# Another order for the hand-written list of four engines: the way back and the first two tiles

## The chip, the cores and the metric

One NeuronCore of a Trainium2 chip runs the kernel. The metric is device time in microseconds (us), the median of several runs. TensorE (PE) multiplies, ScalarE (ACT) and VectorE (DVE) read PSUM and do the elementwise work, GpSimd (POOL) works on SBUF alone, and SyncE (SP) issues the DMAs.

## The reference

A block of two layers on `x` of 2048 x 512, float32: a filter in the frequency domain, then a gated MLP, both with a LayerNorm ahead and a residual.

```python
X = rfft2(layernorm(x)) * (w_r + 1j * w_i)
h = x + irfft2(X, (2048, 512))
g, u = layernorm(h) @ w_gate, layernorm(h) @ w_up     # 512 x 1376 each
out = h + (gelu(g) * u) @ w_down                      # 1376 x 512
```

## The kernel before

The two Fourier transforms are matrix products with tables of sines and cosines. A first stage (to about 32 us) takes the LayerNorm and the transform over the sequence, a second (to about 75 us) does the transform over the columns, the filter and half of the way back; it leaves its result in the SBUF tile `gh`, 16 blocks of 128 rows. A third stage, the subject here, takes the blocks through the rest of the way back and begins the MLP. The MLP then runs in 22 tiles (two halves of the rows, 11 slices of 128 of the 1376 hidden columns, the last one padded), and the products with `w_down` are put between them. TensorE is to be fed all the time.

Products of the MLP are made by a scheme with seven products in place of eight (as Strassen's), and each product is three passes in `fp32r` of 2 x 128 rows (lines 100 to 102: high by high, high by low, low by high parts). So activations (`cb`) and weights (`gu`, `wd`) lie in SBUF as a high and a low part.

In the third stage the order of the instructions on PE, ACT, DVE and POOL is written out by hand. `FIRST` is a list of 292 words; each word is one step, and a loop issues them in the order of the list:

```python
with tc.manual_schedule(engines={et.PE, et.Activation, et.DVE, et.Pool}):
    for op in FIRST.split():
        name, *place = op.split(".")
        do[name](*map(int, place))
```

Each engine runs its own steps in the list's order and waits by semaphores for what it needs of the others. SP's DMAs are not in the list. The number behind the dot is a PSUM bank (of eight) or a spare row in SBUF. The names, with a block `b` or a pair `i` of blocks (i and i+4):

| step | engine, line | what it does |
|---|---|---|
| `U b`, `C b`, `V b`, `X b`, `M b` | PE 524, ACT 844 (811 for b over 7), DVE 852, POOL 881, PE 862 (859/860 for b = 3, 7) | a block's way back: product over the columns, copy out, fold by sum and by difference, product over the sequence |
| `O b`, `H b`, `G b`, `I b` | ACT 867, DVE 873, POOL 877 | half of it copied out, residual, the two halves of the block put together |
| `S b`, `A b`, `E i`, `Q i`, `N i`, `R i` | DVE 514, 516, 895, ACT 908, DVE 900 to 902, ACT 906 | second LayerNorm of a pair |
| `T i0`, `T i1`, `a i` to `o i` | PE 557, 563; ACT 568 to 579, DVE 576, 582, POOL 576, 582 | transposes, and the sums, differences, high and low parts in `cb` that the seven products need |
| `K b` | POOL 818 to 821 | a later block unfolded, four instructions |
| `g n h P0` to `P6` | PE 100 to 102 | the seven products of tile n (0, 1), half h (a: pairs 0, 1; b: pairs 2, 3), 256 columns wide |
| `g n h c1, c2, c3` | ACT 660 | copies of the sum so far, between the products that add to it |
| `d1, d2, dy` / `G0, G1` / `m0, m1` / `i0, i1` / `o0, o1` | DVE 663 / ACT 666 / DVE 669 / ACT 675 / DVE 682 | sums, gelu, gate times up, high and low part for the next product |
| `g n awh`, `g n awl` | ACT 503, POOL 505 | high and low part of a slice of `w_down`, behind a DMA into `wdr` |
| `r0` to `r3`, `hc`, `lo1` to `lo3` | POOL 138 to 146, DVE 153, POOL 156 | weights of tile 2: four sums in `raw`, the high part of all of it, the low part in three pieces |
| `g2P0` | PE | the first product of tile 2, 512 columns wide |

A tile holds its three running sums x, y, z in three banks: tile 0 in banks 0 to 2, tile 1 in 3 to 5, tile 2 again in 0 to 2. P0 starts x and `c1` copies it; P2, P4 and P5 add to x, and each waits until the copy before it (`c1`, `c2`, `c3`) has read x. `dy` adds `c3`'s copy and z to y, and P6 adds to z behind it. The pair's transposes T20, T21, T30, T31 go through banks 6, 7, 7 and 5, which other steps use before and after.

Of the kernel before, what the change touches and what calls it, by code (L numbers as in the profile page):

```python
# [31 lines left out]
BY_THEN = (8, 12, 9)  # L32

FIRST = """
u4.0 u0.1 w4 C4.0 w0 C0.1 U1.2 U5.3 V4.2 X4 V0.3 C1.4 V1.0 C5.5 X0 M4.1 V5.1 X1 O4.0 X5 M0.2 H4 U2.3 O0.1 G4 I4
M5.1 C2.5 H0 V2.3 G0 S4 U7.2 M1.3 O5.0 A4 U6.0 I0 U3.4 X2 H5 C7.1 S0 O1.1 A0 H1 M2.1 C6.0 Q0 C3.5 E0.5 N0 G5
U12.3 R01 V7.4 I5 T01.2 G1 I1 V6.3 S5 X7 A5 R00 T00 S1 O2.1 M7.0 X6 s0.0 A1 a0 Q1 l0 V3.1 E1.6 c0 d0 f0 b0 U8.4
U9.7 N1 e0.1 m0 g0 H2 h0 R10 k0 T10 R11 H7 n0 T11.1 X3 a1 s1.2 b1 c1 i0 d1 j0 l1 M3.2 C8 S7 g0aP0 o0 M6.4 e1.0
h1 f1 U14.5 k1 C12 i1 m1 n1 O6.0 g1 g0ac1 U15.3 H3 j1 S3 C15 r0 o1 A3 g0aP1 C9 A7 g0aP2 Q3 C14 G2 H6 g0ac2 E3.7 I2
N3 g0aP3 G6 U10.4 g0aP4 R31 S2 I6 R30 g0ad1 g0ac3 A2 S6 T31.5 A6 T30 s3.6 g0aP5 g1aP0 a3 Q2 E2.6 g0ady c3 C10  # L40
g0aP6 d3 b3 N2 f3 r1 g1ac1 g3 e3.4 K9.5 g1aP1 R20 r2 h3 g1aP2 i3 g1ad1 g1aP3 k3 R21 j3 T20 T21.7 g1ac2 a2 b2
s2.8 c2 g1aP4 g1ac3 l3 g1aP5 g0bP0 K12.4 d2 m3 g0ad2 n3 f2 g1ady g1aP6 e2.7 g2 g0bP1 o3 k2 l2 m2 g0bc1 h2 n2 i2
g0bd1 j2 g0bP2 g0bP3 g0bc2 o2 g1aG0 r3 g0awh K8.4 g0bP4 U11.6 g0bc3 g1am0 g0bG0 g0bdy g0bP5 g0bm0 g0aG0 g1ad2
g0am0 g1bP0 g0aG1 g0bP6 g0am1 g1bP1 g1bc1 g1ai0 g1aG1 g0bd2 g0awl hc g0bi0 g1bP2 g1bc2 g1bd1 g0bo0 g1bP3 g0ai0
g1bP4 g0bG1 g1bc3 g0ai1 g1bP5 g0ao0 g1ao0 lo1 g0bm1 g0ao1 g2P0 g1awh g0bi1 g1bdy g0bo1 g1am1 g1bP6 lo2 g1bG0
g1ai1 g1bm0 g1bd2 g1ao1 g1awl g1bG1 lo3 g1bm1 g1bi0 g1bo0 g1bi1 g1bo1 U13.7 C11 C13
"""

SECOND = """
# [1121 lines left out]
```

## Time and profile before

| | |
|---|---|
| median of 3 runs | 454.15 us (454.14 to 454.22) |
| the profiled execution's own time | 454.05 us |
| its span, first to last instruction | 452.3 us |
| granted TensorE clock, mean | 0.998 |
| PE, PEld, DVE, ACT, POOL busy | 97%, 82%, 61%, 45%, 61% of the span |

The profiled execution is 0.10 us below the median, and 1.75 us of it lie outside the span. The third stage runs from 75.8 us (the first `U`) to 127.9 us (the end of `U13`, the last PE step of the list). A row of the timeline gives the start, the duration, the engine, the line, the operation, and in brackets the idle time ahead of it with what ended it. Matmuls are pipelined, so the distance from one start to the next, not the duration, is what one costs on PE.

### The profile page before, as it was taken

Reading aid. Unit: us, or ns where it says so; the run is one execution under the profiler, and the core shown is the slowest. Engines: PE = TensorE matmul, PEld = TensorE weight load, DVE = VectorE, ACT = ScalarE, POOL = GpSimd, SP = SyncE. Lnnn points to the kernel's source line nnn. Section 1 sums busy time; section 2 is a strip of 40 time slices with the busy share of each in tenths; the row PEclk is TensorE's granted clock in tenths of the full one; section 3 lists DMA queues with packets and bytes.
Section 4 is the critical chain, followed back from the end, with each engine's and each line's share of the span. In section 5 each row is a group of like instructions: output and inputs, shape, how many; then the busy total and the mean of one; then the engine's idle time right before and its main releaser. Section 6 shows DMA issues by size and latency. Waiting matters only on the chain.

```text
span 452.3 us, 6433 instructions
## 1 busy us (share of the span) xinstructions
PE 437.8 (97%) x2289; PEld 371.1 (82%) x2289; DVE 277.1 (61%) x514; ACT 205.6 (45%) x433; POOL 276.5 (61%) x306
## 2 busy tenths in 40 slices
PE   3999999999999999999999999999999999999996
PEld 3999999798878777877888888888888888888875
DVE  5957895797574766358735578266555345635453
ACT  4979785688731242033332765252243034303420
POOL 6986896878859578748662543165566636653210
PEclk9999999999999999999999999999999999999999
DMA  8994805200032022112210213121022102210013
GB/s 288 390 400 147 278 13 179 100 23 1 25 116 93 26 69 93 48 46 71 70 48 23 70 48 116 49 91 46 26 70 71 46 24 71 70 46 25 23 70 118
DMA packets 21168, 41.05 MB, mean 91 GB/s; under 512 B 2064, under 2 KB 7696, under 8 KB 21008
## 3 DMA queue, kind: packets, MB, share of 16 engines
q1 hardware_dynamic: 20992, 40.51, 26.3%
q8 instruction: 18, 0.29, 0.3%
q10 hardware_dynamic: 144, 0.13, 0.1%
q14 instruction: 14, 0.11, 0.1%
HBM read 36.44 MB, written 4.19 MB: 90 GB/s over the span
## 4 chain that ended last, share of the span: by engine, by line
PE 90%; DVE 3%; ACT 2%; DMA 2%; POOL 1%; issue 1%; SPq 0%; POOLq 0%; DVEq 0%
PE ps L756 26%; PE ps L100 15%; PE ps L102 14%; PE ps L101 14%; PE ps L288 4%; PE ps L416 3%; PE ps L427 3%; PE ps L454 3%; PE ps L524 3%; PE ps L862 1%; PE ps L971 1%; DMA gh<-in_x 1%; POOL gu L156 1%; PE ps L563 1%; DMA raw<-in_wgu 1%; PE ps L557 1%
## 5 line engine op out<-in xcount | busy, mean ns | idle before, releaser
L100 PE MATMUL ps<-cb,gu 128*128 128x512 f32 (+1 forms) x336 | 127.9, 381 | 2.0 <-ACT s L660 1.6
L756 PE MATMUL ps<-wd,a 128*128 128x512 f32 (+1 forms) x537 | 125.9, 388 | 0.2 <-DVE gh L759 0.2
L102 PE MATMUL ps<-cb,gu 128*128 128x512 f32 (+1 forms) x336 | 125.0, 372 | 0.0
L101 PE MATMUL ps<-cb,gu 128*128 128x512 f32 (+1 forms) x336 | 124.9, 372 | 0.0
L756 PEld LDWEIGHTS ps<-wd,a 128*128 128x128 f32 x537 | 99.4, 188 | 21.9 <-DVE gh L972 1.0
L156 POOL TENSOR_TENSOR gu<-raw,gu 128x768 fp32r<-128x768 f32 (+1 forms) x54 | 78.3, 1479 | 39.6 <-DVE gu L153 33.4
L660 ACT ACTIVATE s<-ps 128x512 f32<-128x512 f32 (+1 forms) x72 | 40.4, 560 | 133.8 <-PE ps L102 133.5
L100 PEld LDWEIGHTS ps<-cb,gu 128*128 128x128 f32 x336 | 63.3, 188 | 14.9 <-ACT s L660 2.2
L101 PEld LDWEIGHTS ps<-cb,gu 128*128 128x128 f32 x336 | 63.3, 188 | 11.7 <-issue 1.0
L102 PEld LDWEIGHTS ps<-cb,gu 128*128 128x128 f32 x336 | 63.3, 188 | 11.0
L762 DVE TENSOR_TENSOR gh<-ps,gh 128x512 f32<-128x512 f32 x48 | 33.1, 691 | 53.7 <-PE ps L756 53.5
L505 POOL TENSOR_TENSOR wd<-wdr,wd 128x512 fp32r<-128x512 f32 x22 | 28.4, 1291 | 51.3 <-ACT wd L503 51.2
L669 DVE TENSOR_TENSOR ps<-ps,s 128x512 f32<-128x512 f32 (+1 forms) x48 | 31.0, 650 | 24.4 <-PE ps L102 22.2
L675 ACT ACTIVATE a<-ps 128x512 fp32r<-128x512 f32 (+1 forms) x48 | 26.9, 561 | 39.0 <-DVE ps L669 38.6
L682 DVE TENSOR_TENSOR a<-ps,a 128x512 fp32r<-128x512 f32 (+1 forms) x48 | 30.8, 641 | 11.5 <-ACT a L675 9.8
L663 DVE TENSOR_TENSOR s<-ps,s 128x512 f32<-128x512 f32 (+1 forms) x48 | 30.9, 643 | 10.6 <-PE ps L102 9.1
L666 ACT ACTIVATE s<-s 128x512 f32<-128x512 f32 (+1 forms) x48 | 28.2, 592 | 18.4 <-DVE s L663 18.4
L138 POOL TENSOR_TENSOR raw<-raw 128x256 f32<-128x256 f32 x20 | 14.7, 737 | 33.9 <-DMA raw<-in_wgu 32.4
L663 DVE TENSOR_TENSOR ps<-ps,s 128x512 f32<-128x512 f32 (+1 forms) x24 | 15.7, 654 | 27.8 <-ACT s L660 27.8
L288 PE MATMUL ps<-ms,pn 128*128 128x128 f32 x120 | 17.0, 291 | 7.9 <-ACT ms L256 7.8
L288 PEld LDWEIGHTS ps<-ms,pn 128*128 128x128 f32 x120 | 15.6, 205 | 8.3 <-POOL pn L263 7.2
L153 DVE CAST gu<-raw 128x1792 fp32r<-128x1792 f32 x18 | 19.6, 1091 | 3.8 <-PE ps L101 2.9
(126 smaller groups left out, 609.5 us busy)
## 6 DMA issues: line engine op xcount, KB each, us to landing
raw<-in_wgu SPq DMA_DIRECT2D x40, 256.0 KB, 3.1
wt<-in_w SPq DMA_DIRECT2D x16, 520.0 KB, 5.7
wdr<-in_wd SPq DMA_DIRECT2D x22, 256.0 KB, 2.7
out<-gh SPq DMA_DIRECT2D x15, 256.0 KB, 2.0
gh<-in_x SPq DMA_DIRECT2D x7, 512.0 KB, 8.1
row<-in_x SPq DMA_DIRECT2D x12, 256.0 KB, 3.0
mis<-in_mi SPq DMA_DIRECT2D x1, 1024.0 KB, 10.6
a<-in_x SPq DMA_DIRECT2D x4, 256.0 KB, 4.9
```

What stands on the lines that cost most here:

```text
L100: pe.matmul(o, lh, rh, start=(i == 0 and not onto), stop=False, skip_group_check=True)
L101: pe.matmul(o, lh, rl, start=False, stop=False, skip_group_check=True)
L102: last = pe.matmul(o, ll, rh, start=False, stop=(i == n - 1), skip_group_check=True)
L156: pooled["lo"] = pool.tensor_tensor(r[:, 1, m], t[:, m], r[:, 0, m].bitcast(F32), op=ALU.subtract)
L288: pe.matmul(pt[:, c], o, mc, start=(z == 0), stop=(z == len(parts[b][c]) - 1))
L505: pool.tensor_tensor(r[:, 1], t, r[:, 0].bitcast(F32), op=ALU.subtract)
L660: return lambda: act.activation(to, a, AF.Copy)
L663: return lambda: dve.tensor_tensor(to, a, b, op=ALU.add)
L669: return lambda: dve.tensor_tensor(u, u, g, op=ALU.mult)
L682: dve.tensor_tensor(a[:, 1], u, a[:, 0].bitcast(F32), op=ALU.subtract)
L756: pe.matmul(o, parts_of[tiles.index((q, f))][:, ha, i // 4, r], wds[f][:, hw, c], start=start, stop=stop)
L762: dve.tensor_tensor(gh[:, b, c], o, gh[:, b, c], op=ALU.add)
```

## The change

Only the list `FIRST` changes: the same 292 words, with the same banks and rows behind the dots, in another order. Its first and its last rows:

```diff
-u4.0 u0.1 w4 C4.0 w0 C0.1 U1.2 U5.3 V4.2 X4 V0.3 C1.4 V1.0 C5.5 X0 M4.1 V5.1 X1 O4.0 X5 M0.2 H4 U2.3 O0.1 G4 I4
+u4.0 u0.1 w4 C4.0 w0 C0.1 U1.2 C1.4 U5.3 V4.2 X4 V0.3 X0 V1.0 X1 C5.5 V5.1 X5 r0 M4.1 O4.0 M0.2 O0.1 H4 G4 U2.3 C2.5
...
-g1ai1 g1bm0 g1bd2 g1ao1 g1awl g1bG1 lo3 g1bm1 g1bi0 g1bo0 g1bi1 g1bo1 U13.7 C11 C13
+g0bG1 g0bm1 U11.6 C11 g1bP5 g1ao0 g1bP6 g1bd2 g0bi1 g0bo1 g1bG1 U13.7 C13 g2P0 g1bm0 g1bi0 g1bm1 g1bi1 g0ao1 g1bo0
+g1bo1 g1ao1
```

On PE the order of the products from the first of them on was, and is now (the steps with P; with U, T and M between):

```
before: g0aP0 M6 U14 U15 g0aP1 g0aP2 g0aP3 U10 g0aP4 T31 T30 g0aP5 g1aP0 g0aP6 g1aP1 g1aP2 g1aP3 T20 T21 g1aP4 g1aP5
        g0bP0 g1aP6 g0bP1 g0bP2 g0bP3 g0bP4 U11 g0bP5 g1bP0 g0bP6 g1bP1 g1bP2 g1bP3 g1bP4 g1bP5 g2P0 g1bP6 U13
after:  U15 T10 M6 T11 M3 g0aP0 U14 U10 g0aP2 g0aP1 g1aP0 g0aP4 T31 g1aP2 T30 g1aP1 g1aP4 g0aP3 g0aP5 T20 g1aP5 T21 g0aP6
        g0bP0 g1bP1 g1bP0 g1aP3 g0bP1 g0bP2 g1aP6 g0bP3 g0bP4 g1bP2 g0bP5 g0bP6 g1bP3 g1bP4 U11 g1bP5 g1bP6 U13 g2P0
```

ACT, around the loading of the table for gelu (line 666's first row). `s1_907`, `s2_908`, `s3_909` are the copies of tile 0, `s1_910`, `s2_911` those of tile 1; `wd` is the high part of `w_down`; before:

```order
L660 ACTIVATE s1_907<-ps_72 128x256
L579 ACTIVATE cb_885<-row_893 128x2x128
L579 ACTIVATE cb_885<-ps_72 128x2x128
L660 ACTIVATE s2_908<-ps_72 128x256
L666 ACT_TABLE_LOAD
L666 ACTIVATE s1_910<-s1_910 128x256
L503 ACTIVATE wd_1331<-wdr_1329 128x512
L660 ACTIVATE s3_909<-ps_72 128x256
L666 ACTIVATE s1_907<-s1_907 128x256 x2
```

and now:

```order
L660 ACTIVATE s1_907<-ps_72 128x256
L579 ACTIVATE cb_885<-row_892 128x2x128
L666 ACT_TABLE_LOAD
L666 ACTIVATE s1_907<-s1_907 128x256
L660 ACTIVATE s2_908<-ps_72 128x256
L666 ACTIVATE s2_908<-s2_908 128x256
L579 ACTIVATE cb_885<-ps_72 128x2x128
L579 ACTIVATE cb_885<-row_894 128x2x128
L666 ACTIVATE s2_911<-s2_911 128x256
L660 ACTIVATE s3_909<-ps_72 128x256
```

The load now stands ahead of `g0bc2` (`s2_908`) and no longer between it and `g0bc3` (`s3_909`); `g0awh` (`wd`) has left this place for one 59 steps earlier in ACT's order (behind `O1`).

POOL, at the end of the list. `cb` are the steps `m` and `o`, `wd` is `g0awl` or `g1awl`, `gu` are `lo1` to `lo3`, the four rows with `gh` are `K8`; before:

```order
L576 TENSOR_TENSOR row_893<-row_894 128x256
L582 TENSOR_TENSOR cb_885<-row_894,cb_885 128x2x128
L582 TENSOR_TENSOR cb_885<-row_893,cb_885 128x2x128
L146 TENSOR_TENSOR raw_915<-raw_915 128x256
L818 TENSOR_TENSOR row_893<-gh_58 128x2x128
L819 TENSOR_TENSOR row_893<-gh_58 128x2x128
L820 TENSOR_TENSOR gh_58<-row_893 128x256
L821 TENSOR_TENSOR gh_58<-row_893 128x256
L505 TENSOR_TENSOR wd_1331<-wdr_1329,wd_1331 128x512
L156 TENSOR_TENSOR gu_82<-raw_915,gu_82 128x256
L156 TENSOR_TENSOR gu_82<-raw_915,gu_82 128x768
L505 TENSOR_TENSOR wd_1434<-wdr_1432,wd_1434 128x512
```

and now:

```order
L146 TENSOR_TENSOR raw_915<-raw_915 128x256
L582 TENSOR_TENSOR cb_885<-row_893,cb_885 128x2x128
L818 TENSOR_TENSOR row_893<-gh_58 128x2x128
L819 TENSOR_TENSOR row_893<-gh_58 128x2x128
L820 TENSOR_TENSOR gh_58<-row_893 128x256
L821 TENSOR_TENSOR gh_58<-row_893 128x256
L582 TENSOR_TENSOR cb_885<-row_892,cb_885 128x2x128
L582 TENSOR_TENSOR cb_885<-row_894,cb_885 128x2x128
L505 TENSOR_TENSOR wd_1372<-wdr_1370,wd_1372 128x512
L156 TENSOR_TENSOR gu_82<-raw_915,gu_82 128x256
L156 TENSOR_TENSOR gu_82<-raw_915,gu_82 128x768 x2
```

`m3` and `m2`, the low parts that P6 of half b needs, now stand behind `K8`; `g1awl` stands ahead of all three low parts of tile 2's weights.

DVE, around the high part of tile 2's weights (the CAST, `hc`); before:

```order
L669 TENSOR_TENSOR ps_72<-ps_72,s1_907 128x256
L669 TENSOR_TENSOR ps_72<-ps_72,s2_908 128x256
L663 TENSOR_TENSOR s2_908<-ps_72,s2_908 128x256
L153 CAST gu_82<-raw_915 128x1792
L663 TENSOR_TENSOR s1_910<-ps_72,s1_910 128x256
L682 TENSOR_TENSOR a_1388<-ps_72,a_1388 128x256 x2
```

and now:

```order
L669 TENSOR_TENSOR ps_72<-ps_72,s1_910 128x256
L669 TENSOR_TENSOR ps_72<-ps_72,s1_907 128x256
L153 CAST gu_82<-raw_915 128x1792
L669 TENSOR_TENSOR ps_72<-ps_72,s2_911 128x256
L663 TENSOR_TENSOR s2_908<-ps_72,s2_908 128x256
L669 TENSOR_TENSOR ps_72<-ps_72,s1_907 128x256
L663 TENSOR_TENSOR ps_72<-ps_72,s3_912 128x256
```

`hc` now stands ahead of `g0bd2` (`s2_908`), and `g1bdy` (`s3_912`), for which `g1bP6` waits, four steps behind it. `hc` writes over the weights of tile 0, so it can start only behind `g0bP6`, in both orders.

More of the change, by code (lines that the diff above doesn't have):

```diff
@@ L34 @@
 FIRST = """
-u4.0 u0.1 w4 C4.0 w0 C0.1 U1.2 U5.3 V4.2 X4 V0.3 C1.4 V1.0 C5.5 X0 M4.1 V5.1 X1 O4.0 X5 M0.2 H4 U2.3 O0.1 G4 I4
[L36 to L44, printed above, removed]
@@ L45 @@
-g1bP4 g0bG1 g1bc3 g0ai1 g1bP5 g0ao0 g1ao0 lo1 g0bm1 g0ao1 g2P0 g1awh g0bi1 g1bdy g0bo1 g1am1 g1bP6 lo2 g1bG0
-g1ai1 g1bm0 g1bd2 g1ao1 g1awl g1bG1 lo3 g1bm1 g1bi0 g1bo0 g1bi1 g1bo1 U13.7 C11 C13
+u4.0 u0.1 w4 C4.0 w0 C0.1 U1.2 C1.4 U5.3 V4.2 X4 V0.3 X0 V1.0 X1 C5.5 V5.1 X5 r0 M4.1 O4.0 M0.2 O0.1 H4 G4 U2.3 C2.5
+M5.1 I4 O5.0 H0 U7.2 G0 C7.1 V2.3 M1.3 I0 O1.1 S4 g0awh X2 H5 G5 A4 S0 A0 E0.5 Q0 U3.4 C3.5 H1 U6.0 C6.0 M2.1 N0 R00
+R01 U12.3 C12 V7.4 I5 S5 A5 V6.3 U8.4 I1 G1 O2.1 T00 a0 S1 T01.2 A1 Q1 E1.6 X7 M7.0 U9.7 H2 N1 s0.0 c0 d0 C8 R10 g0awl
@@ new lines @@
+H7 e0.1 k0 n0 b0 h0 f0 g0 R11 S7 X6 U15.3 V3.1 X3 l0 i0 j0 T10 a1 b1 I2 G2 m0 M6.4 O6.0 T11.1 s1.2 c1 d1 C15 o0 C9 f1
+e1.0 k1 n1 H6 I6 M3.2 g0aP0 H3 g0ac1 o1 l1 U14.5 C14 m1 U10.4 C10 g1 g0aP2 g0aP1 S3 A3 A7 Q3 g1aP0 h1 i1 g0ac2 g0aP4
+E3.7 N3 R31 T31.5 G6 S6 g1ac1 g1aP2 K12.4 R30 T30 K9.5 S2 A2 g1aP1 A6 E2.6 Q2 s3.6 N2 c3 d3 g1ac2 g1aP4 g0aP3 R21 a3
+e3.4 g0ac3 j1 g0aP5 R20 T20 g1ac3 g1aP5 b3 h3 i3 g0ad1 g1ad1 j3 k3 T21.7 r1 r2 g0ady g0aP6 a2 b2 g0bP0 g1bP1 n3 s2.8
+c2 d2 f3 g3 e2.7 k2 n2 h2 f2 g2 g1bP0 g1bc1 g1aP3 g1ady g0bc1 l3 o3 g0bP1 g0bd1 g0bG0 g0bP2 g0bc2 g0ad2 r3 g1aP6 g1ad2
@@ L47 @@
+g0aG1 g0bP3 i2 j2 g0am1 l2 g1aG1 o2 g0bP4 g0bc3 g0bdy K8.4 g1bd1 g1aG0 g1bP2 g1bc2 g1awh g1am0 g1ai0 g0bP5 g0bm0 g0bi0
+m3 m2 g0bP6 g1bP3 g1bG0 g1awl hc lo1 lo2 lo3 g0aG0 g1am1 g0bd2 g1bP4 g1bc3 g0am0 g0ai0 g0ai1 g1bdy g0ao0 g0bo0 g1ai1
+g0bG1 g0bm1 U11.6 C11 g1bP5 g1ao0 g1bP6 g1bd2 g0bi1 g0bo1 g1bG1 U13.7 C13 g2P0 g1bm0 g1bi0 g1bm1 g1bi1 g0ao1 g1bo0
+g1bo1 g1ao1
 """
```

## The prediction

> **What bounds the kernel now.** I read the page first, then the busy time by stretches, then the timeline of PE in the third stage, and last that of the engines it waits for.
>
> ```profile
> PE 437.8 (97%) x2289; PEld 371.1 (82%) x2289; DVE 277.1 (61%) x514; ACT 205.6 (45%) x433; POOL 276.5 (61%) x306
> 75.70:128.00 52.30, 50.14 (x364) 44.68 (x364) 37.71 (x97) 38.08 (x90) 41.34 (x54) 1.00 0.17 55
> 140.00:450.00 310.00, 308.56 (x1373) 253.57 (x1371) 172.72 (x281) 105.84 (x194) 164.80 (x164) 1.00 0.19 60
> ```
>
> PE is the bound, and behind the changed stretch it is idle for 1.4 us of 310. So what PE gains or loses up to 128 us reaches the end of the span, and a reordering can win only what PE loses in the stretch. Busy time understates that loss, because a matmul's modelled end covers part of a gap. I take distances between starts. The rows come in the order of time, those of the six places where PE stood still among them:
>
> ```profile
> 81.17 1.05 PE L524 MATMUL ps<-dis,gh 128*128 128x128 f32 x8
> 82.06 1.02 PE L862 MATMUL ps<-row,mis 128*128 128x512 f32 x2
> ...
> 102.87 0.60 PE L563 MATMUL ps<-ident,a 128*128 128x128 f32 x4
> 103.31 0.60 PE L557 MATMUL ps<-ident,a 128*128 128x128 f32 x4
> ...
> 107.10 0.28 PE L101 MATMUL ps<-cb,gu 128*128 128x256 f32 x1
> 107.22 0.28 PE L102 MATMUL ps<-cb,gu 128*128 128x256 f32 x1
> 107.65 0.39 PE L100 MATMUL ps<-cb,gu 128*128 128x256 f32 x1
> 107.87 0.28 PE L101 MATMUL ps<-cb,gu 128*128 128x256 f32 x1
> ...
> 108.46 0.60 PE L557 MATMUL ps<-ident,a 128*128 128x128 f32 x4
> 109.14 0.66 PE L563 MATMUL ps<-ident,a 128*128 128x128 f32 x4
> ...
> 110.23 0.28 PE L102 MATMUL ps<-cb,gu 128*128 128x256 f32 x1
> 110.99 0.39 PE L100 MATMUL ps<-cb,gu 128*128 128x256 f32 x1 [0.47 <-ACT s L660]
> ...
> 116.13 1.05 PE L524 MATMUL ps<-dis,gh 128*128 128x128 f32 x8
> 117.83 0.39 PE L100 MATMUL ps<-cb,gu 128*128 128x256 f32 x1 [0.65 <-ACT s L660]
> ...
> 119.36 0.28 PE L100 MATMUL ps<-cb,gu 128*128 128x256 f32 x1
> ...
> 122.86 0.28 PE L102 MATMUL ps<-cb,gu 128*128 128x256 f32 x1
> 123.61 0.39 PE L100 MATMUL ps<-cb,gu 128*128 128x256 f32 x1 [0.47 <-ACT s L660]
> ...
> 124.43 0.39 PE L100 MATMUL ps<-cb,gu 128*128 128x512 f32 x1
> 124.66 0.39 PE L101 MATMUL ps<-cb,gu 128*128 128x512 f32 x1
> ...
> 125.58 0.40 PE L102 MATMUL ps<-cb,gu 128*128 128x512 f32 x1
> 126.25 0.38 PE L100 MATMUL ps<-cb,gu 128*128 128x256 f32 x1 [0.26 <-DVE ps L663]
> ...
> 127.06 1.05 PE L524 MATMUL ps<-dis,gh 128*128 128x128 f32 x8
> 127.87 0.47 PE L100 MATMUL ps<-cb,gu 128*128 128x512 f32 x1
> ```
>
> A matmul of 256 columns costs 0.12 us (107.10 to 107.22), so a product of six costs 0.72, and from its first start to its last end 0.88 (five times 0.12 and 0.28). A `U` costs 0.89 (81.17 to 82.06), a transpose step 0.44 (102.87 to 103.31), a product of 512 columns 6 x 0.23 = 1.40. The six losses: `g1aP3` at 107.65, where 107.34 was due: 0.31. `T21` at 109.14, due 108.90: 0.24. `g1aP5` at 110.99, due 110.35: 0.64. `g0bP5` at 117.83, due 117.02: 0.81. `g1bP5` at 123.61, due 122.98: 0.63. `g1bP6` at 126.25, due 125.81: 0.44. Together 3.07. In five of them the first matmul costs 0.22 instead of 0.12 (107.65 to 107.87), 0.50 more. **PE loses 3.57 us in six waits**, and that bounds the gain.
>
> **The waits that go.** No operation is added or removed; each term is a wait. Three are loops through ACT: a product ends, ACT copies its sum, the next product may add to it.
>
> ```profile
> L844 ACT ACTIVATE row<-ps 128x512 f32<-128x512 f32 x8 | 4.7, 596 | 3.9 <-PE ps L524 3.9
> L660 ACT ACTIVATE s<-ps 128x256 f32<-128x256 f32 x12 | 4.6, 381 | 3.1 <-PE ps L102 2.9
> ...
> 115.28 1.28 ACT L666 ACT_TABLE_LOAD   x1
> 116.57 0.42 ACT L666 ACTIVATE s<-s 128x256 f32<-128x256 f32 x1
> 116.89 0.61 ACT L503 ACTIVATE wd<-wdr 128x512 fp32r<-128x512 f32 x1
> 117.41 0.36 ACT L660 ACTIVATE s<-ps 128x256 f32<-128x256 f32 x1
> ```
>
> Such a loop takes 0.88 of product, 0.38 of copy and about 0.1 of two hand-overs (the copy ends at 117.77, PE starts at 117.83): 1.36 us from start to start. One product between the two gives PE 2 x 0.72 = 1.44 us and just hides it; nothing between does not.
>
> - `g1aP5` (0.64) and `g1bP5` (0.63) stood directly behind P4. Now `g1aP4` is followed by `g0aP3`, `g0aP5` and `T20` (1.88 us of other work) and `g1bP4` by `U11` (0.89). Both waits go.
> - `g0bP5` (0.81): its copy stood behind the table load, a gelu and `g0awh`, 2.1 us from 115.28 to 117.41. Now the load stands ahead of `g0bc2`, and `g0awh` stands among the blocks' copies, ahead of which ACT idles for 3.9 us in eight places (line 844). The load now threatens `g0bc2`. With `g0bP4` due at 115.45 (below), `g1bP0`, six products earlier, is due at 111.13, and ACT copies its sum from 112.05 on. `g0bc1`, `l3`, the load, a gelu and `g0bc2` follow: 112.05 + 3 x 0.38 + 2 x 0.42 + 1.28 = 115.3. It clears by 0.1.
> - `g1aP3` (0.31): its bank still held a transpose that ACT and DVE were reading. It now comes behind `g0bP0`, `g1bP1` and `g1bP0`, 2.2 us later. `T21` (0.24): `g1aP5` now lies between it and `T20`, 0.72 us. Both go.
> - `g1bP6` (0.44): it waited for `g1bdy` on DVE (the bracket names its line, 663). This one may come back.
>
> **What is late next.** In the new order `g0bP6` has two more products (`g1bP1`, `g1bP2`) ahead of it and one `U` less: 119.36 + 1.44 - 0.89, less the first four waits (2.00 and three slow first matmuls, 0.30), is 117.61. Three products earlier, at 115.45, stands `g0bP4`; `g1bP6` is due at 117.61 + 4 x 0.72 + 0.89 = 121.38. On the other side stand `hc` and `g1awl`:
>
> ```profile
> 119.59 0.76 DVE L669 TENSOR_TENSOR ps<-ps,s 128x256 f32<-128x256 f32 x2
> 120.62 1.08 DVE L153 CAST gu<-raw 128x1792 fp32r<-128x1792 f32 x1
> 121.62 0.42 DVE L663 TENSOR_TENSOR s<-ps,s 128x256 f32<-128x256 f32 x1
> ...
> 113.41 1.44 POOL L582 TENSOR_TENSOR cb<-row,cb 128x256 fp32r<-128x256 f32 x2
> ...
> 115.51 0.74 POOL L818 TENSOR_TENSOR row<-gh 128x256 f32<-128x256 f32 x1
> ...
> 118.40 1.29 POOL L505 TENSOR_TENSOR wd<-wdr,wd 128x512 fp32r<-128x512 f32 x1
> 121.85 2.54 POOL L156 TENSOR_TENSOR gu<-raw,gu 128x256 fp32r<-128x256 f32 x2 [2.17 <-DVE gu L153]
> ...
> L582 DVE TENSOR_TENSOR cb<-ps,cb 128x512 fp32r<-128x512 f32 x8 | 5.5, 686 | 1.2 <-ACT cb L579 0.9 <-ACT row L573 0.3
> ```
>
> Before, `hc` ran from 120.62 with POOL idle (2.17 us, up to 121.85). Now `hc` may start when `g0bP6` ends, at 118.5. `g1awl` (1.29) follows `g1awh` on ACT: copy, gelu, copy and `g1awh` behind `g0bP4`'s end bring it to about 118.0, so it runs to 119.3. The two overlap, which the trace of before does not show. The bounds: `hc` loses nothing, or waits 0.9 us until `g1awl` is done. I take the wait, by the nearest row: the CAST moves 1792 columns in 1084 ns, 0.6 ns a column, the DVE's other rows 512 in 686, 1.3 a column. It has twice the ordinary access to SBUF, and that must come from somewhere.
>
> The Trainium skill, page "SBUF — State Buffer", section "Who interferes with whom", says where: a VectorE copy in its two-port mode and a GpSimd instruction exclude each other, and the one that starts second fully blocks. By it `hc` starts at 119.3 too; no run here shows it yet.
>
> With the wait, `hc` starts at 119.4, takes 1.00 (120.62 to 121.62), and three steps of 0.34 (half of 0.76, less the tail) lead to `g1bdy`, which ends at 121.84. `g1bP6` starts at 121.9 instead of 121.38: 0.5, and 0.1 for its first matmul. Then P1 of tile 2 waits for `g0ao1`, nine DVE steps behind `g1bdy`, several of them gated by ACT: 121.42 + 9 x 0.34 + 0.42 = 124.9 at the earliest, about 125.3 with ACT's part, against 125.0 for PE: 0.3. Two margins of 0.1 to 0.2 (`g0bP4`, `g0bP5`) get 0.2 together, and 0.1 goes to the slow first matmul behind P1's wait. New losses: 1.2.
>
> **Off the path.** `g0awl` (1.29) moves ahead of `k0` on POOL, which costs nothing as long as POOL would wait there for `s0` anyway; without that cover `M3`, which needs `X3` four POOL steps later, is late by 1.29 at most. `g0awh`'s DMA was issued long before. `K8`, `lo1` to `lo3` and with them the DMA of tile 3's weights, which SP issues once `lo3` has read `raw`, end two to three microseconds earlier, as PE does, so nothing is given back there. I found no place ahead of 105 us where an operand is due less than 0.5 us before PE.
>
> **The sum.** 454.05 - 3.57 + 1.2 = 451.7 for the profiled execution; the median stood 0.10 above it: **451.8 us**. A measurement of this kernel can tell about 0.2%, 0.9 us, from no change.
>
> **The rivals.**
>
> 1. `hc` and `g1awl` run side by side. Then `g1bdy` ends at 121.0, both new waits fall to the 0.2 of the margins, and the time is 454.05 - 3.57 + 0.2 + 0.1 = 450.8. For it: POOL's rows keep 0.73 to 0.75 us beside all DVE work. Against it: the CAST's rate.
> 2. ACT is late at the loops with little cover. Five of them (`g0aP4`, `g1aP4`, `g0aP5`, `g0bP4`, `g0bP5`) clear by 0.1 to 0.6; if ACT, which has more queued ahead of each, is 0.4 late in all five, 2.0 us come back: 453.8, within 0.2% of before. For it: every wait that I remove was such a small one. Against it: a late PE gives the other engines time, so such losses don't all add.
> 3. Slower: POOL becomes the bound at `m2`. Before, `m2` ran at 113.41, was done by 114.15, and `g0bP6` came at 119.36: 5.2 us of slack. Now `o3`, `r3`, `o2`, all of `K8` (115.51 to 118.40, 2.89) and `m3` stand between: from `T21`'s start 0.66, 0.7 for `s2` on ACT, and 6 x 0.70 + 2.89, together 8.5, against 0.44 + 12 x 0.72 = 9.1 for PE. The slack is 0.6; every microsecond beyond it is PE's, and 3.3 more make it slower than before by 0.9: 455.1. For it: POOL has no gap left in that run. Against it: the 7.1 us of POOL would have to become 11.
>
> **How the numbers follow.** The forecast has 0.54, rival 1 0.25, rival 2 0.13, rival 3 0.08. Rival 2 counts half as faster, since not all five need fail. Faster by over 0.2%: 0.54 + 0.25 + 0.06 = 0.85; within: 0.07; slower: 0.08. The low end is all of the 3.57 won, 454.15 - 3.57 = 450.6; the high end, 453.2, lets rival 2's five places fail by 0.28 each on top of the forecast.
>
> **What would show it.** Right: `g2P0`'s last matmul ends PE's list near 125.3 instead of 127.9; none of the waits at `g1aP3`, `T21`, `g1aP5`, `g0bP5` and `g1bP5` is left above 0.2; `hc` starts just as `g1awl` ends, and `g1bP6` shows an idle time ended by DVE line 663. Wrong: `hc` starts inside `g1awl`'s row (rival 1), idle times at the copies of line 660 (rival 2), or `g0bP6` ended by POOL line 582 (rival 3). A gain at 128 us that is gone at 450 would refute the reading that PE carries it to the end.

## The result, and the profile after

The changed order takes 450.85 us (median of 6 runs, 450.76 to 450.97) against 454.14 (6 runs, 453.93 to 454.27): ratio 0.9926, interval 0.9916 to 0.9937, 3.29 us faster. The forecast was 451.8 with a range of 450.6 to 453.2; it was 0.95 too high. The profiled execution took 450.89 us, its span is 449.1.

The page after, engines and the groups of lines 100 and 153:

```profile
PE 436.8 (97%) x2289; PEld 371.1 (83%) x2289; DVE 277.4 (62%) x514; ACT 205.2 (46%) x433; POOL 276.3 (62%) x306
...
L100 PE MATMUL ps<-cb,gu 128*128 128x512 f32 (+1 forms) x336 | 127.6, 380 | 0.3 <-DVE ps L663 0.2
...
L153 DVE CAST gu<-raw 128x1792 fp32r<-128x1792 f32 x18 | 20.4, 1133 | 4.9 <-PE ps L101 2.3
```

The same work was done (the instruction counts of the engines are those of before). The busy time by stretches, PE first:

```profile
75.70:128.00 52.30, 51.95 (x377) 46.97 (x377) 40.85 (x102) 40.31 (x96) 41.26 (x54) 1.00 0.23 71
```

PE is busy for 51.95 of the 52.30 us in which it was busy for 50.14 before. What PE waited for, from the view of waits (total, times, longest), without the two waits that lie ahead of the third stage:

```profile
PE ps L756 <- DVE gh L759: 0.2, 1, 0.2
PE ps L100 <- DVE ps L663: 0.2, 1, 0.2
```

No wait for ACT's copies (line 660) is left. The timeline, first PE at the end of the list, then POOL, DVE and ACT:

```profile
120.05 0.36 PE L100 MATMUL ps<-cb,gu 128*128 128x256 f32 x1
121.16 0.38 PE L100 MATMUL ps<-cb,gu 128*128 128x256 f32 x1 [0.16 <-DVE ps L663]
...
124.02 0.40 PE L102 MATMUL ps<-cb,gu 128*128 128x512 f32 x1
124.54 0.50 PE L100 MATMUL ps<-cb,gu 128*128 128x512 f32 x1
124.88 0.39 PE L101 MATMUL ps<-cb,gu 128*128 128x512 f32 x1
...
117.53 1.29 POOL L505 TENSOR_TENSOR wd<-wdr,wd 128x512 fp32r<-128x512 f32 x1 [0.93 <-ACT wd L503]
...
117.94 1.84 DVE L153 CAST gu<-raw 128x1792 fp32r<-128x1792 f32 x1 [0.21 <-PE ps L101]
119.69 0.42 DVE L669 TENSOR_TENSOR ps<-ps,s 128x256 f32<-128x256 f32 x1
...
120.69 0.42 DVE L663 TENSOR_TENSOR ps<-ps,s 128x256 f32<-128x256 f32 x1
...
124.07 1.42 DVE L682 TENSOR_TENSOR a<-ps,a 128x256 fp32r<-128x256 f32 x4
...
112.55 1.28 ACT L666 ACT_TABLE_LOAD   x1
...
114.17 0.36 ACT L660 ACTIVATE s<-ps 128x256 f32<-128x256 f32 x1
```

Two new waits are there. `g1bP6` starts at 121.16 where 120.84 was due (its first matmul then costs 0.10 more), just behind `g1bdy` (DVE, ends at 121.11). P1 of tile 2 starts at 124.54 where 124.25 was due (and 0.11), just behind `g0ao1` (the first of the four at 124.07). Together 0.83. Ahead of both stands `hc`: a row of 1.84 us where the same CAST took 1.08 before.

There is a gain that the prediction's sum doesn't have. The transposes of the first two pairs, with their neighbours, before:

```profile
88.22 0.66 PE L563 MATMUL ps<-ident,a 128*128 128x128 f32 x4
88.84 0.66 PE L557 MATMUL ps<-ident,a 128*128 128x128 f32 x4
89.33 0.60 PE L859 MATMUL ps<-row,mis 128*128 128x256 f32 x2
...
91.06 1.95 PE L524 MATMUL ps<-dis,gh 128*128 128x128 f32 x16
92.92 0.66 PE L557 MATMUL ps<-ident,a 128*128 128x128 f32 x4
93.54 0.66 PE L563 MATMUL ps<-ident,a 128*128 128x128 f32 x4
94.03 0.60 PE L859 MATMUL ps<-row,mis 128*128 128x256 f32 x2
```

and after:

```profile
89.18 0.60 PE L557 MATMUL ps<-ident,a 128*128 128x128 f32 x4
89.62 0.60 PE L563 MATMUL ps<-ident,a 128*128 128x128 f32 x4
90.06 0.60 PE L859 MATMUL ps<-row,mis 128*128 128x256 f32 x2
...
91.79 1.95 PE L524 MATMUL ps<-dis,gh 128*128 128x128 f32 x16
93.57 0.60 PE L557 MATMUL ps<-ident,a 128*128 128x128 f32 x4
94.01 1.02 PE L862 MATMUL ps<-row,mis 128*128 128x512 f32 x2
```

A transpose step cost 0.62 and 0.49 from start to start at the first pair before (88.22, 88.84, 89.33), 0.62 and 0.49 again at the second, and the two `U` ahead of it 1.86 instead of 1.78; after, each step costs 0.44 and the two `U` 1.78. That is 0.18 + 0.05 + 0.08 + 0.18 + 0.05 = 0.54: three transposes that start late (by 0.18, 0.08 and 0.18), and 0.05 more in the step behind two of them. The timeline of PE marks none of it with a bracket. The timeline of before marks the two longer ones at the transposes' weight loads (PEld):

```profile
88.83 0.42 PEld L557 LDWEIGHTS ps<-ident,a 128*128 128x128 f32 x4 [0.20 <-ACT a L906]
...
93.54 0.42 PEld L563 LDWEIGHTS ps<-ident,a 128*128 128x128 f32 x4 [0.19 <-ACT a L906]
```

They waited for `R`, the normalized rows that ACT makes: before, the two `R` of the first pair had ended at 88.79 and `T00` started at 88.84; after, they have ended at 88.55 and `T00` starts at 89.18, behind one more `U`.

So the account closes: -3.57 (six waits) - 0.54 (transposes) + 0.83 (two new waits) = -3.28. Summed over all PE starts from 75 to 140 us, what a distance is longer than the usual one of its kind (less what others are shorter) makes 4.89 us before and 1.65 after, 3.24 less; the medians differ by 3.29.

### The profile page after: what moved, and what is told of

Same layout as the page of the kernel before. It is cut to its first block, busy times and chain, and to the rows that moved or that the text cites. A ratio compares the mean times of both kernels' runs of the same rounds, so it can differ in the third digit from the quotient of the medians.

```text
span 449.1 us, 6433 instructions
## 1 busy us (share of the span) xinstructions
PE 436.8 (97%) x2289; PEld 371.1 (83%) x2289; DVE 277.4 (62%) x514; ACT 205.2 (46%) x433; POOL 276.3 (62%) x306
## 4 chain that ended last, share of the span: by engine, by line
PE 95%; DVE 2%; DMA 1%; ACT 1%; issue 0%; SPq 0%; DVEq 0%
PE ps L756 26%; PE ps L100 15%; PE ps L101 15%; PE ps L102 15%; PE ps L288 5%; PE ps L416 3%; PE ps L427 3%; PE ps L454 3%; PE ps L524 3%; PE ps L971 1%; PE ps L862 1%; DMA gh<-in_x 1%; PE ps L557 1%; PE ps L563 1%; DVE ps L669 1%; DVE gu L153 0%
```

## The experiments

Eleven runs; each shared its chip with runs of the kernel before, whose median was 454.26 to 454.32 there. "Against before" is the difference of the two medians; the order after has -3.29. "PE's excess" is the sum just described, from the profile.

| run | changed order | median, us | ratio to before, interval | against before | PE's excess |
|---|---|---|---|---|---|
| (after) | | 450.85 | 0.9926, 0.9916 to 0.9937 | -3.29 | 1.65 |
| e1 | after | 450.08 | 0.9908, 0.9895 to 0.9922 | -4.20 | 0.77 |
| e2 | after | 450.01 | 0.9907, 0.9894 to 0.9921 | -4.27 | 0.75 |
| e3 | after | 451.93 | 0.9951, 0.9938 to 0.9965 | -2.35 | 2.67 |
| e4 | after | 451.98 | 0.9949, 0.9937 to 0.9962 | -2.30 | 2.38 |
| e6 | after | 449.77 | 0.9901, 0.9888 to 0.9915 | -4.50 | 0.49 |
| e7 | after | 451.86 | 0.9946, 0.9934 to 0.9959 | -2.41 | 2.67 |
| e8 | after | 451.52 | 0.9937, 0.9925 to 0.9950 | -2.75 | 2.37 |
| (before) | | 454.14 | | 0 | 4.89 |
| e5 | before | 454.23 | 1.0000, 0.9991 to 1.0009 | -0.04 | 4.96 |
| e9 | before | 454.19 | 0.9999, 0.9990 to 1.0008 | -0.07 | 4.92 |
| e10 | before | 453.39 | 0.9981, 0.9972 to 0.9990 | -0.87 | 4.18 |
| e11 | before | 453.11 | 0.9974, 0.9964 to 0.9983 | -1.21 | 3.88 |

The intervals of e1, e2, e4, e7 and e8 overlap or touch that of the order after, e8's most. That these five differ from it rests on PE's excess and on the rows below, and not on the medians alone.

### Does `g1awl` hold `hc`? (e1, e2)

e1 takes POOL's instruction out of the CAST's way, e2 lets it come second (its operand `g1awh`, on ACT, is made later):

```diff
 e1: -... m3 m2 g0bP6 g1bP3 g1bG0 g1awl hc lo1 lo2 lo3 g0aG0 ...
     +... m3 m2 g0bP6 g1bP3 g1bG0 hc lo1 lo2 lo3 g1awl g0aG0 ...
 e2: -... g1bc2 g1awh g1am0 g1ai0 g0bP5 g0bm0 g0bi0 m3 ...
     +... g1bc2 g1am0 g1ai0 g0bP5 g0bm0 g0bi0 g1awh m3 ...
```

> The changed list with one word moved: g1awl behind lo3, so that POOL has nothing to do while hc runs. Theory (the copy hc and a POOL instruction exclude each other; hc starts at 117.94 and takes 1.83 us because g1awl holds it until 118.82): hc takes 1.09 us again, as in the other 17 tiles, the waits of 0.42 at g1bP6 and 0.41 at P1 of tile 2 are gone, and the time is 450.85 - 0.8 = 450.0 to 450.2 us. Rival (hc is slow because of what PE and ACT read at that time): hc still takes about 1.8 us, both waits stay, 450.8 us.

> The changed list with one word moved: g1awh behind g0bi0 on ACT, so that g1awl becomes ready at about 118.7 us, when hc, from 117.94 on, already runs. Theory (whoever starts first holds the other off for all of its time): hc takes 1.09 us, g1awl starts or ends as if it had started at hc's end, about 119.0, and the time is 450.1 to 450.3 us. Rival (the two share, and both get slower while they overlap): hc takes 1.3 us or more, and the time is 450.4 to 450.7 us.

The timeline of e1, the CAST:

```profile
117.64 1.09 DVE L153 CAST gu<-raw 128x1792 fp32r<-128x1792 f32 x1 [0.21 <-PE ps L101]
```

and of e2:

```profile
117.91 1.09 DVE L153 CAST gu<-raw 128x1792 fp32r<-128x1792 f32 x1 [0.21 <-PE ps L101]
...
118.72 1.42 POOL L505 TENSOR_TENSOR wd<-wdr,wd 128x512 fp32r<-128x512 f32 x1 [2.14 <-ACT wd L503]
```

In both the CAST takes 1.09, and both new waits of PE are gone. In e2 the two still meet, and it is POOL's row that is longer, 1.42 instead of 1.29; PE doesn't wait for that one. So the later of the two pays, whichever engine it is on. The Trainium skill, page "SBUF — State Buffer", section "Who interferes with whom", says that of a VectorE instruction in its two-port mode and a GpSimd instruction the first gets the shared pair of ports for the whole instruction and the other fully blocks. The traces of after and e2 agree, and in e1, where the two lie apart, neither is longer. After `g1awl`'s end (118.82) the CAST ran for 0.96 us more, after the CAST's end in e2 (119.00) `g1awl` ran for 1.14: nearly all of their work lay behind the other's end.

### Are PE's waits worth what their distances say? (e3, e4, e7, e8)

Four ways to put a wait back into the order after. e3: `g1aP5` directly behind `g1aP4` again. e4: the table load (with `g0bG0`) behind `g0bc2`. e7: rival 3's slack, with three sums of tile 2's weights between `K8` and `m3`. e8: the cover of the first transposes taken away.

```diff
 e3: -... g1aP4 g0aP3 R21 a3 e3.4 g0ac3 j1 g0aP5 R20 T20 g1ac3 g1aP5 b3 ...
     +... g1aP4 R21 a3 e3.4 g1ac3 j1 g1aP5 g0aP3 g0ac3 g0aP5 R20 T20 b3 ...
 e4: -... g0bP1 g0bd1 g0bG0 g0bP2 g0bc2 g0ad2 r3 ...
     +... g0bP1 g0bd1 g0bP2 g0bc2 g0bG0 g0ad2 r3 ...
 e7: -... T21.7 r1 r2 g0ady ... g0ad2 r3 g1aP6 ... g0bm0 g0bi0 m3 m2 g0bP6 ...
     +... T21.7 g0ady ... g0ad2 g1aP6 ... g0bm0 g0bi0 r1 r2 r3 m3 m2 g0bP6 ...
 e8: -... N0 R00 R01 U12.3 C12 V7.4 I5 S5 A5 V6.3 U8.4 I1 G1 O2.1 T00 a0 S1 T01.2 A1 ...
     +... N0 R01 R00 U12.3 C12 V7.4 I5 S5 A5 V6.3 I1 G1 O2.1 T00 a0 S1 T01.2 U8.4 A1 ...
```

> The changed list with one of the old neighbourhoods restored: g1aP5 stands directly behind g1aP4 again, with its copy g1ac3 ahead of g0ac3 on ACT and g0aP3 behind it. Theory (a product directly behind the one whose sum must be copied waits 1.36 - 0.72 = 0.64 us, and its first matmul costs 0.10 more): one idle time of 0.7 us at g1aP5, ended by ACT line 660, nothing else new, 451.5 to 451.6 us. Rival (PE makes such a wait good later, since all else has slack): 450.9 us.

> The changed list with g0bc2 ahead of g0bG0 on ACT, so that the table load of 1.28 us stands between g0bc2 and g0bc3 again, as before the change. Theory (the load's place made the largest of the old waits): g0bc3 ends at about 117.1 instead of 116.2, g0bP5 waits 0.8 us for it and its first matmul costs 0.10 more, 451.6 to 451.8 us. Rival (it was g0awh in that place, not the load, which ACT can hide): under 0.3 us at g0bP5, 450.9 to 451.1 us.

> The order after with r1, r2 and r3 (weights of tile 2, 0.73 us each on POOL) moved behind K8, directly ahead of m3 and m2. The prediction gave m2 a slack of 0.6 us on POOL; the trace of the order after has m2's end at 116.60 and g0bP6 at 117.08, 0.48. r3 stood ahead of m2 already, so m2 is 1.47 us later if POOL had no idle time behind T20, and g0bP6 waits about 1.0 and 0.1: 451.8 to 451.95 us, with an idle time of PE ended by POOL line 582. Rival: POOL has idle time between that takes r1 and r2, m2 isn't late: 450.9 us.

> The order after with T00's cover taken away: R00 behind R01 on ACT, and U8 behind T01 and no longer ahead of T00. By the trace of the order after T00 would be due at about 88.2 and R00 end at 88.56. Theory: the prediction's missing term is this cover, PE waits about 0.4 at the transpose and does not get it back: 451.2 to 451.3 us. Rival: a small wait so early is made good later, since the other engines gain the time: 450.9 us.

The rows that answer, in the timeline of e3 (PE, DVE):

```profile
106.21 0.39 PE L100 MATMUL ps<-cb,gu 128*128 128x256 f32 x1 [0.47 <-ACT s L660]
...
110.05 0.28 PE L100 MATMUL ps<-cb,gu 128*128 128x256 f32 x1
110.48 0.38 PE L101 MATMUL ps<-cb,gu 128*128 128x256 f32 x1
...
109.73 0.69 DVE L582 TENSOR_TENSOR cb<-ps,cb 128x512 fp32r<-128x512 f32 x1 [1.35 <-ACT cb L579]
```

of e4 (ACT, PE):

```profile
114.29 1.28 ACT L666 ACT_TABLE_LOAD   x1
...
117.09 0.37 ACT L660 ACTIVATE s<-ps 128x256 f32<-128x256 f32 x1
...
117.52 0.39 PE L100 MATMUL ps<-cb,gu 128*128 128x256 f32 x1 [0.79 <-ACT s L660]
```

of e7 (POOL, PE, DVE):

```profile
117.06 1.42 POOL L582 TENSOR_TENSOR cb<-row,cb 128x256 fp32r<-128x256 f32 x2
118.43 1.30 POOL L505 TENSOR_TENSOR wd<-wdr,wd 128x512 fp32r<-128x512 f32 x1
...
118.53 0.39 PE L101 MATMUL ps<-cb,gu 128*128 128x256 f32 x1 [1.22 <-POOL cb L582]
...
119.37 1.31 DVE L153 CAST gu<-raw 128x1792 fp32r<-128x1792 f32 x1 [1.69 <-PE ps L101]
```

and of e8 (PE, ACT):

```profile
89.02 0.66 PE L557 MATMUL ps<-ident,a 128*128 128x128 f32 x4 [0.15 <-ACT a L906]
...
87.65 1.32 ACT L906 ACTIVATE a<-gh,rs 128x512 f32<-128x512 f32 x2
```

Each wait came where it was expected. Against the order after, by the differences to before:

- e3: 0.94 slower, 0.7 expected. Besides the loop (0.63 + 0.10) there is a second wait, 0.31 + 0.10 at 110.48: the copies stand in another order on ACT (the likely cause), a low part in `cb` (DVE line 582, gated by ACT) ends only at 110.42, and a product goes on at 110.48. It wasn't foreseen.
- e4: 0.99 slower, 0.75 to 0.95 expected. `g0bP5` waits 0.95 + 0.10 for a copy that the load has delayed; `g1bP6`'s wait shrinks from 0.32 to 0.18 meanwhile. PE's excess is only 0.73 over that of after. 0.19 of the rest lies ahead of the third stage, where nothing was changed: its first `U` starts at 76.05 here and at 75.86 in the order after.
- e7: 0.88 slower, 0.95 to 1.1 expected. `m2` ends 1.88 us later than after (118.48 for 116.60), and PE waits 1.38 + 0.11 for it: 0.50 of slack, near the 0.6 that the prediction gave POOL. The wait was 1.49, the loss smaller: `g1bP6` no longer waits (0.42 before), since `hc`, 1.4 us later too, overlaps less of `g1awl` and loses 0.22 instead of 0.75. PE's excess is 1.02 over that of after.
- e8: 0.54 slower (0.67 by the medians alone), 0.35 to 0.45 expected. T00 waits 0.32, with 0.06 behind it, and it is not made good later. Only this 0.38 belongs to the cover. The profile has 0.21 + 0.07 at `M5` (82.48 us) too, ahead of the moved steps. `M5` writes the bank that `H4` reads, and `H4`, on DVE, waited for the DMA of `x`:

```profile
81.59 1.41 DVE L873 SCALAR_TENSOR_TENSOR a<-a,mv,ps 128x512 f32<-128x512 f32 x2 [0.60 <-DMA a<-in_x]
```

In the order after this row starts at 81.01, behind ACT and not behind a DMA. So the gap at `M5` is most likely a late DMA and none of the moved steps. The profiled execution (451.88) is the slowest of e8's five; whether the others have that gap is not known.

### A fill alone, in the order before (e5, e9, e10, e11)

The prediction said of `g1bP5` that a `U` between it and `g1bP4` hides its loop. That can be done in the order before by moving one word:

```diff
 e5:  -... g0ai0 g1bP4 g0bG1 g1bc3 g0ai1 g1bP5 ... g1bi1 g1bo1 U13.7 C11 C13
      +... g0ai0 g1bP4 U13.7 g0bG1 g1bc3 g0ai1 g1bP5 ... g1bi1 g1bo1 C11 C13
 e9:  before, -... g1bd1 g0bo0 g1bP3 ... g1bP5 g0ao0 g1ao0 lo1 ...
              +... g1bd1 g0bo0 g1ao0 g1bP3 ... g1bP5 g0ao0 lo1 ...
 e10: e5 and e9 together
 e11: e5, and g1ao0 behind U13:  ... g1bP4 U13.7 g1ao0 g0bG1 g1bc3 g0ai1 g1bP5 g0ao0 lo1 ...
```

> The order before, with one step moved: U13 stands directly behind g1bP4, so it lies between g1bP4 and g1bP5 and no longer at the list's end. Waits are local and additive: g1bP5's loop of 1.36 us gets 0.89 of cover, its wait of 0.63 and the slow first matmul (0.10) go, g1bP5 itself starts 0.26 later and g1bP6 still waits for g1bdy, at most as long as before. PE wins 0.6 to 0.75: 453.4 to 453.6 us. Rival: a wait that is filled turns up at another place, because ACT or DVE hold the rate of this stretch: 454.2 us, with the six waits' sum near 3.57 as before.

The time did not move (454.23 against 454.27). `g1bP5`'s wait was gone, and 0.34 + 0.11 stood at P1 of tile 2 and 0.21 + 0.11 at line 756 (137.06 us, behind DVE line 762) in its place: 0.77 for 0.73. The 453.4 to 453.6 that was expected is refuted; the rival's number, 454.2, was met. The timeline of e5, PE, then DVE and ACT:

```profile
127.77 0.50 PE L100 MATMUL ps<-cb,gu 128*128 128x512 f32 x1 [0.18 <-DVE a L682]
...
127.29 0.42 DVE L682 TENSOR_TENSOR a<-ps,a 128x256 fp32r<-128x256 f32 x1 [0.73 <-ACT a L675]
...
126.39 0.60 ACT L660 ACTIVATE s<-ps 128x512 f32<-128x512 f32 x1 [1.81 <-PE ps L102]
126.88 0.38 ACT L675 ACTIVATE a<-ps 128x256 fp32r<-128x256 f32 x1
```

P1 waits for `g0bo1` on DVE (127.29), which waits for `g0bi1` on ACT (126.88), which stands behind the copy of tile 2's first sum (126.39). That was there before too, but `U13` covered it. Why was ACT's step so late? One row of before, on DVE:

```profile
124.63 0.43 DVE L682 TENSOR_TENSOR a<-ps,a 128x256 fp32r<-128x256 f32 x1 [1.38 <-PE ps L102]
```

That is `g1ao0`, of half a, and it stands idle until `g1bP5`, of half b, has ended: the sums x of half a and half b are the two halves of one bank, and the list has `g1bP5` first. `g0bm1`, `g0ao1` and `g1bdy` are queued behind it. e9 to e11 move it.

> The order before, with one step moved: g1ao0 (DVE 682) directly behind g0bo0 and no longer behind g1bP5. In the trace of before DVE stands idle for 1.38 us at g1ao0 until g1bP5's last matmul has ended, and g0ao0's successors, g1bdy among them, queue behind it. Theory: a wait of PE goes where the queue of the engine that releases it is made free: g1bdy ends 1.1 us earlier, g1bP6's 0.44 and the slow first matmul (0.10) go, 453.7 us. Rival: g1bdy then waits for something else (ACT's c3, the sum z) until the same time: 454.2 us.

> The order before with both moves: U13 directly behind g1bP4 (alone, in e5_fill_before, it brought nothing: P1 of tile 2, which had U13 as its cover, waited 0.34 instead) and g1ao0 directly behind g0bo0 (DVE isn't held by g1bP5 any more, and the copy of tile 2's first sum stands behind g0bi1 and a gelu on ACT, no longer ahead of g0bi1). Theory: with DVE free, what the filled loop gives isn't asked for again by P1: g1bP5's 0.73 and g1bP6's 0.54 both go, 453.0 us, or up to 453.3 if line 756 at 136 us waits 0.2 to 0.3 as in e5_fill_before. Rival: the filled wait comes back whatever DVE does, so only what e9_dve_free wins is left: 453.7 us.

> The order before, U13 directly behind g1bP4 and g1ao0 directly behind U13 (in e9_dve_free and e10_fill_and_free it stood ahead of g1bP4, which adds to the bank that it reads and so waited 0.52 + 0.10 for it). Theory: g1ao0 now follows g1bP4's end on DVE and is done ahead of g1bP5; none of the waits at g1bP4, g1bP5, g1bP6 and P1 of tile 2 is left, 453.0 us (454.27 less 0.73 and 0.54). Rival: another wait takes their place, 453.4 us as in e10_fill_and_free, or more.

e9, PE:

```profile
122.90 0.39 PE L100 MATMUL ps<-cb,gu 128*128 128x256 f32 x1 [0.36 <-DVE a L682]
```

`g1bP6`'s wait went, as the theory had it, and the time didn't (454.19): `g1ao0` now stood ahead of `g1bP4`, which adds to the same bank and waited 0.52 + 0.10 for it. That I had overlooked. The rival's 454.2 was met, but not by its reason; neither expectation names this wait. With it still there, e10 misses its 453.0 to 453.3 a little and is 0.80 us faster than e9 through `U13` alone (453.39), so the fill that was worth nothing in e5 is worth its 0.73 once DVE isn't held. In e11 `g1ao0` stands behind `g1bP4` and the gain is 1.21, 1.27 expected. What is left there is 0.21 + 0.10 at `g1bP5`, by the row on ACT for `g1bc3` (below, behind DVE's row that begins with `g1ao0`):

```profile
123.30 0.76 DVE L682 TENSOR_TENSOR a<-ps,a 128x256 fp32r<-128x256 f32 x2 [0.80 <-PE ps L102]
...
123.76 0.38 ACT L660 ACTIVATE s<-ps 128x256 f32<-128x256 f32 x1 [0.54 <-DVE a L682]
```

ACT's copy out of the bank waits for DVE's read of its other half, a read behind a read. The Trainium skill, page "PSUM — Partial Sum Buffer", section "PSUM bank collisions raise a hardware error", tells of a scheduler that puts a dependency between any two instructions of different engines on the same bank (and the same quarter of its partitions), ACT against DVE too, whether they touch the same columns or not. The three waits (`g1ao0` for P5, P4 for `g1ao0`, `g1bc3` for `g1ao0`) agree with it. Which of the two comes first in the list decides who waits, and that has a price on both sides.

### What is left (e6)

```diff
 e6 = e1, and for tile 2 the two running steps `ending` (line 971 on PE, 972 on DVE) one step earlier, ahead of its P2:
+            early_lates = n == 2
+            if early_lates:
+                for g in ending:
+                    next(g)
             step(n)
...
-            for g in ending:
-                next(g)
+            if not early_lates:
+                for g in ending:
+                    next(g)
```

> The order after with g1awl behind lo3 (as in e1_awl_last, 450.08 us), and the running sums that end tile 2's products (line 971, DVE) are issued one step of the schedule earlier, ahead of its P2. Theory: what is left of PE's waits is the 0.21 + 0.11 at line 756, behind DVE line 972; with DVE's sums earlier it goes, 449.75 us. Rival: DVE isn't free any earlier, or the steps push others behind them: 450.1 us.

449.77 us, as forecast, 1.21 below the order after by the differences to before. The wait at line 756 is gone; what is left of PE's excess is 0.49, of which 0.33 is the start of the stage. That is the fastest version here.

## Why the prediction was right or wrong

- **What bounds the kernel: right.** The gain in the stretch reached the end in full: 3.24 by PE's starts, 3.29 by the medians.
- **The waits that go: right in the sum, incomplete in one reason.** All six are gone, 3.57. Of `g1bP5` the text says that `U11` hides its loop; e5 shows that in the order before a `U` there gives nothing, because P1 of tile 2 then asks for the same time. In the order after `g1bdy` stands ahead of `g1ao0` on DVE, and so it isn't held until `g1bP5` ends; e10 shows that a fill counts when DVE isn't held. I read the wait at `g1bP6` as one for `g1bdy` and didn't ask why `g1bdy` was late, though the 1.38 us of idle DVE stood in the timeline.
- **The term that is missing: 0.54.** The 3.57 of the six waits is not what "bounds the gain", as the prediction has it: the transposes gave 0.54 more, and e1 and e2, where the two new waits are gone, come out below its low end of 450.6. "I found no place ahead of 105 us where an operand is due less than 0.5 us before PE" looked for what the change might make late there, not for what it frees. Before, `R` on ACT held three of the first four transposes by 0.08 to 0.18 each. e8 shows the other side of that cover: without it PE waits 0.32 for `R`, 0.38 with what follows, of the 0.54 by which the time is longer.
- **What is late next: right in the mechanism, too large by 0.37 (1.2 for 0.83).** `g1awl` does hold `hc`, and `g1bP6` and P1 of tile 2 pay, as written (e1, e2: 0.91 and 0.98 faster without). Of the 1.2, `g1bP6` got 0.5 + 0.1 and took 0.32 + 0.10: from `g1awl`'s end to DVE's step behind `hc` the prediction has a hand-over of 0.1 and 1.00, together 1.1; the trace has 0.87 (118.82 to 119.69). P1's 0.3 + 0.1 was met (0.30 + 0.11). The margins' 0.2 was not needed: `g0bc2` ended at 114.53, `g0bP4` was due at 114.92, 0.39 of room where I had 0.1.
- **The signs.** "`hc` starts just as `g1awl` ends" was wrong, and so was the sign for rival 1, "`hc` starts inside `g1awl`'s row": `hc` does start inside it, 0.41 us after its start, and is held all the same. By those two sentences alone the trace would have given the case to the rival. `g2P0`'s last matmul ended PE's list at 124.42, not near 125.3: the missing 0.54, the 0.18 at `g1bP6` and the 0.2 of margins are about what it came early.
- **Rival 1** came within 0.05 us in number (450.8), by luck, since the missing 0.54 stood against new waits that it did not have; it is refuted in its mechanism: with the two really apart the time is 450.0 to 450.1.
- **Rival 2** did not happen: no wait for line 660 is left. e4 shows what it would have cost at one place, 0.99. **Rival 3** did not happen, and its slack was read well: 0.50 in e7 for 0.6.

## What to carry to other kernels

A wait on the bounding engine is worth its length only if whoever is next has that much room: fill one gap, then look for the next wait behind it, and follow its releaser's queue back to where that engine itself stood idle. Add up distances between starts over the whole stretch for what is lost, since the waits of 0.08 to 0.18 us at the transposes carry no mark in PE's timeline, and with what they cost behind them made 0.54 of the 4.1 that were won. Where two engines must share a bank or a port, the order of the list decides who pays, so put the work that nobody waits for second.

## What the runs showed that was not expected

- A blocked instruction shows as a longer row, not as a later one: the CAST 1.84 us instead of 1.08 when it starts 0.41 us behind POOL's, 1.31 when it starts 0.94 us behind it (e7); in both it ends 0.95 to 0.96 us after POOL's row. POOL's, as the later one, 1.42 instead of 1.29, for 0.28 us of overlap. No bracket marks any of this: those on these rows name other waits.
- A copy by ACT stood idle for 0.54 us until a read by DVE of the same bank had ended (e11).
